# Windowed attention with a routed expert network on one Trainium2 core: other transfer sizes and places for v and the first w1, conversions behind copies, spin matmuls in the start

## The chip, the core and the metric

The kernel runs on one core of a Trainium2 chip. The time is device microseconds of one execution, from the first to the last activity of the core. The kernel before took 225.32 us (median of 3 runs, 225.25 to 226.03). The profile that is read here is of one more execution, of 225.92 us.

## What is computed

Eight sequences ("batches") of 576 rows go through windowed causal attention with 8 heads of 64 columns. The heads are put side by side into x (576 x 512 per batch). The mean over x's rows picks one of eight experts for the whole batch, and this expert's two matrices turn x into the output.

```python
scores = scale * q @ k.T                     # per batch and head, 576 x 576
scores = where(0 <= row - col < 64, scores, -1e9)
x = softmax(scores) @ v                      # heads side by side: 576 x 512
e = argmax(x.mean(rows) @ w_gate)            # one expert for a batch
out = gate_weight * (relu(x @ w1[e]) @ w2[e])   # w1 512 x 1024, w2 1024 x 512
```

## The kernel before, in words

**Units.** The attention of a batch is cut into two units of four heads; unit u belongs to batch u // 2. `load_qk(u)` fetches q and k of a unit on GpSimd's software DMA queue (they become bf16 on the way). `transpose_qk` turns them on TensorE, `leave_qk` copies the result out of PSUM (q always on ScalarE, k on ScalarE or VectorE), `scores` makes three tiles of scores and their exponentials (ScalarE, L397), `values` multiplies by v, and `norm` divides by the row sums and writes x (VectorE, L439 and L441).

**v.** `load_v(b)` fetches the v of a whole batch, 1.18 MB in runs of 256 bytes, on SyncE's hardware DMA queue, in the order in which SyncE meets the transfers; the stores of the output stand in the same queue. Before each transfer GpSimd writes one element of the tile (`memset`, or a copy from the tile given as `behind`), so that the transfer starts no earlier than that. Three tiles serve for v in turn. The conversion of a unit's half of v to f16 has three parts in `cast_part`: "whole" (vn to va, L323), "low" and "high" (va to vb, shifted by half a block of rows). All of them run on VectorE before the change. The fourth batch's v (b = 3) comes in two transfers: blocks 0 to 19 with `load_v(3, part=20)` at L749, and the rest with `load_rest` at L802, behind the second half of batch 1's w1.

**Gate and experts.** `gate(b)` makes the eight logits with one matmul (gl, L501), copies them to SBUF (glog, L505), takes their maximum and its index on VectorE and hands the index to GpSimd, which loads it into a register and issues the loads of w1 and w2 of that expert. For batches 0 and 1 `load_w1` brings w1 in two halves of 512 columns. `expert_up` makes one of eight blocks of the hidden layer (php, L570; relu on ScalarE, L574), `expert_down` one of five blocks of the output (pso, L584 and L601), copied to ob (L311) and stored.

**Order.** Each engine works through its instructions in the order of the program, and that order is written by hand: a preamble for units 0 to 3 (L707 to L779), then a loop over t = 4 to 19, in which a step holds the attention of unit t and slices of the experts' work (`experts(pace)`). In even steps `next_gate` runs the gate of batch t // 2 - 1. `busy(n)` runs n matmuls on a constant tile, whose result nobody reads. PSUM has four tiles of two banks for everything on TensorE, so a tile can start only when an earlier one has been emptied.

Of the kernel before, what the change touches and what calls it, by code (L numbers as in the profile page):

```python
# [9 lines left out]
FP32 = mybir.dt.float32  # L10
# [146 lines left out]
def kernel(  # L157
# [10 lines left out]
    nc = tc.nc  # L168
    B, H, S, D = q.shape
# [10 lines left out]
    def P(ins):  # L180
        tc.keep_in_program_order(ins)
        return ins
# [33 lines left out]

    v_tiles = {}

    def load_v(b, behind=None, part=0):
        vn = vpool.tile([128, NM, D], FP32, tag="vn")  # L220
        if behind is None:

            P(nc.gpsimd.memset(vn[:, 0, 0:1], 0.0))
        else:

            P(nc.gpsimd.tensor_copy(out=vn[:, 0, 0:1], in_=behind))
        v_tiles[b] = vn
        if part:
            P(nc.sync.dma_start(out=vn[:, 0:part, :], in_=vv[b][:, 0:part, :]))
        else:  # L230
            P(nc.sync.dma_start(out=vn, in_=vv[b]))

    def load_rest(b, part, behind):
        vn = v_tiles[b]
        P(nc.gpsimd.tensor_copy(out=vn[:, part, 0:1], in_=behind))
        P(nc.sync.dma_start(out=vn[:, part:NM, :], in_=vv[b][:, part:NM, :]))

    HM = NM // 2

# [238 lines left out]
    w1e = moe_w1.rearrange("e (g p kl) f -> e p g kl f", p=128, kl=2)  # L478
    w1c = moe_w1.rearrange("e (kb p) f -> e p kb f", p=128)
    w2e = moe_w2.rearrange("e (g p i) d -> e p g i d", p=128, i=4)  # L480

    gparts = {}

# [15 lines left out]
    def gate(b):  # L499
        gl = psum.tile([128, 2, 512], FP32, tag="ps", name="gl")  # L500
        P(nc.tensor.matmul(out=gl[:, 0, 0:E], lhsT=onesf, rhs=gparts[b],  # L501
                           start=True, stop=True))

        glog = small.tile([128, E], FP32, tag="glog")
        P(nc.vector.tensor_copy(out=glog, in_=gl[:, 0, 0:E]))  # L505
        gmx = small.tile([128, 8], FP32, tag="gmx")
        P(nc.vector.max(out=gmx, in_=glog))
# [12 lines left out]
        weights[b] = (wpool.tile([128, KB, F], FP16, tag="w1t", name=f"w1t{b}"),  # L520
                      wpool.tile([128, FB, Dm], FP16, tag="w2t", name=f"w2t{b}"))
# [8 lines left out]

    experts_of = {}

    NQ = 2

    def w1_parts(b):
        return weights[b][0].rearrange("p k f -> p (k f)").rearrange(
            "p (h k f) -> p h k f", h=NQ, k=KB)

    def load_w1(b):
        if b < 2:  # L540

            src = w1c[experts_of[b]].squeeze(0)
            for hf in range(NQ):
                P(nc.gpsimd.dma_start(out=w1_parts(b)[:, hf],
                                      in_=src[:, :, ts(hf, F // NQ)]))
        else:
            P(nc.gpsimd.dma_start(  # L547
                out=weights[b][0].rearrange("p (g kl) f -> p g kl f", kl=2),
                in_=w1e[experts_of[b]].squeeze(0)))

    def load_w2(b):
        P(nc.gpsimd.dma_start(
            out=weights[b][1].rearrange("p (g i) d -> p g i d", i=4),
            in_=w2e[experts_of[b]].squeeze(0)))

    h_tiles = {}

    def expert_up(b, ft):
        if b < 2:
            w1t, cols = w1_parts(b)[:, ft // 4], slice(ft % 4, 512, 4)  # L560
# [157 lines left out]
        scores(0, c)  # L718
    make_masks()
    transpose_qk(1, 0)  # L720
    transpose_qk(1, 1, leave=False)
    leave_qk(1, 1, A)
    load_qk(3)
    load_qk(4)
    cast_v(0)
    cast_v(1)
    for c in range(3):
        add_outside(1, c)
    for c in range(3):
        scores(1, c)  # L730
    values(0, 0)
# [5 lines left out]
    pool_mm(0)  # L737
    transpose_qk(2, 1, leave=False)
    leave_qk(2, 1, A)
    busy(1)  # L740
    pool_mm(1)
    pool_parts()
    gate(0)
    load_w1(0)
    load_w2(0)
    load_qk(5)
    load_v(2, w1_parts(0)[:, 0, 0, 0:1])
    load_qk(6)
    load_v(3, part=20)  # L749
    for c in range(3):  # L750
        scores(2, c)
        if c == 0:
# [28 lines left out]
    for t in range(START + 1, NU + LAG):  # L781
# [3 lines left out]
        def next_gate():  # L785
# [81 lines left out]


# [35 lines left out]
```

## Time and profile before

| what | value |
|---|---|
| time, median of 3 runs | 225.32 us (225.25 to 226.03) |
| the profiled execution | 225.92 us, of which the span is 224.0 us |
| TensorE matmul busy | 201.1 us, 90% of the span |
| ScalarE, VectorE, GpSimd busy | 134.2, 128.6, 39.1 us |
| DMA | 45.64 MB written, mean 204 GB/s |
| mean granted TensorE clock | 0.972 |

All places in time are microseconds from the span's start. In the timeline a row gives start, duration, engine, source line, operation, what it writes and reads, how often (x), and in brackets how long the engine stood idle before it and what ended that. In a table of windows the first columns are the busy time of the engines, then come the granted clock of TensorE, the share of the 16 DMA engines and GB/s. Rows of DMA issues end with the size and the time from issue to landing.

### The profile page before, as it was taken

The numbers are of one execution on the slowest core, as the hardware profiler recorded it, in microseconds if no ns is written. First come the engines' busy times: TensorE is split into PE (matmuls) and PEld (weight loads), VectorE is DVE, ScalarE is ACT, GpSimd is POOL, SyncE is SP. The second block draws the span as 40 slices with busy tenths as digits, with TensorE's granted clock in tenths as the row PEclk, the third lists the DMA queues.
The fourth block names the chain that finished last, engine by engine and source line by source line (L and its number), as shares of the span: only waits on it lengthen the run. The fifth ranks groups of instructions, "written<-read, shape, count | busy, mean of one in ns | idle before, by whom it ended". The sixth has DMA issues, their size and how long they took to land.

```text
span 224.0 us, 6996 instructions
## 1 busy us (share of the span) xinstructions
PE 201.1 (90%) x3012; PEld 141.4 (63%) x3012; DVE 128.6 (57%) x310; ACT 134.2 (60%) x221; POOL 39.1 (17%) x69
## 2 busy tenths in 40 slices
PE   7859759999799897999999999999999998999960
PEld 2437638856586556865696658775777567569520
DVE  2538696557866665576774769395939373330120
ACT  2275695964768464785769476968495656417300
POOL 7170161053000700034000700050002000200000
PEclk9976999999999999999999999999999999999995
DMA  5999899999999999999999999999956990699141
GB/s 69 243 256 246 149 157 219 242 251 235 257 225 203 236 223 244 230 288 217 244 227 277 218 231 235 250 264 219 246 141 113 212 266 5 97 225 263 52 136 41
DMA packets 34310, 45.64 MB, mean 204 GB/s; under 512 B 7136, under 2 KB 26720, under 8 KB 34272
## 3 DMA queue, kind: packets, MB, share of 16 engines
q0 software_dynamic: 14624, 26.22, 65.3%
q1 hardware_dynamic: 18704, 18.75, 28.9%
q8 instruction: 25, 0.41, 0.7%
q10 hardware_dynamic: 944, 0.16, 0.4%
q14 instruction: 13, 0.11, 0.1%
HBM read 61.90 MB, written 9.44 MB: 318 GB/s over the span
## 4 chain that ended last, share of the span: by engine, by line
PE 64%; DMA 12%; ACT 11%; DVE 6%; issue 2%; POOL 1%; POOLq 0%
PE php L570 26%; PE pso L584 20%; DMA w1t<-in_moe_w_dram 8%; PE tp L342 6%; ACT xT L470 5%; DMA kn<-in_k_dram 4%; PE op L425 4%; ACT hT L574 4%; PE sp L382 2%; PE pso L601 2%; ACT pt L397 2%; DVE x L441 1%; PE tp L462 1%; DVE vb L311 1%; PE gl L501 1%
## 5 line engine op out<-in xcount | busy, mean ns | idle before, releaser
L570 PE MATMUL php<-xT,w1t 128*128 128x288 f16 x512 | 70.0, 287 | 3.4 <-DMA w1t<-in_moe_w_dram 2.3
L574 ACT ACTIVATE hT<-php,gatew 128x576 f16<-128x576 f32 x64 | 47.2, 744 | 28.8 <-PE php L570 28.6
L570 PEld LDWEIGHTS <-w1t 128*128 128x128 f16 x512 | 56.0, 115 | 10.0 <-DMA w1t<-in_moe_w_dram 2.9
L584 PE MATMUL pso<-w2t,hT 128*128 128x512 f16 x256 | 60.2, 380 | 0.2
L397 ACT ACTIVATE pt<-sp 128x768 f16<-128x768 f32 x48 | 36.4, 817 | 7.5 <-PE sp L382 7.5
L584 PEld LDWEIGHTS <-hT 128*128 128x128 f16 x256 | 23.3, 98 | 26.1 <-issue 1.2
L311 DVE COPY ob<-pso 128x512 f32<-128x512 f32 x23 | 15.9, 690 | 22.9 <-PE pso L584 22.7
L441 DVE TENSOR_TENSOR x<-op,linv 128x640 f16<-128x640 f32 x32 | 26.4, 825 | 1.1
L404 DVE TENSOR_TENSOR pt<-pt,masks 128x768 f16<-128x768 f16 x42 | 22.6, 554 | 5.7 <-ACT pt L397 4.7
L355 ACT COPY dst<-tp 128x1152 bf16<-128x1152 bf16 x16 | 18.0, 1124 | 11.9 <-PE tp L342 11.7
L547 POOL DMA_DIRECT2D w1t<-in_moe_w_dram x6 | 4.4, 729 | 112.8 <-DVE pt L404 91.5
L470 ACT ACTIVATE xT<-tp 128x576 f16<-128x576 f16 x28 | 17.9, 646 | 9.2 <-PE tp L462 9.2
L425 PE MATMUL op<-vb,pt 128*64 128x65 f16 x320 | 16.2, 198 | 0.8 <-DVE ob L311 0.7
L311 DVE COPY vb<-va 64x1152 f16<-64x1152 f16 (+1 forms) x32 | 15.9, 498 | 0.5
L425 PEld LDWEIGHTS <-pt 128*64 128x64 f16 x640 | 13.9, 114 | 3.3 <-issue 2.4
L425 PE MATMUL op<-va,pt 128*64 128x65 f16 x320 | 15.9, 198 | 0.0
L382 PE MATMUL sp<-dst 64*64 64x128 bf16 (+1 forms) x672 | 14.2, 218 | 1.9 <-ACT dst L309 1.2
L382 PEld LDWEIGHTS <-dst 64*64 64x64 bf16 x672 | 10.3, 110 | 8.7 <-issue 4.5
L311 DVE CAST va<-vn 128x1152 f16<-128x1152 f32 x16 | 12.2, 763 | 6.2 <-DMA vn<-in_v_dram 6.1
L493 DVE SCALAR_TENSOR_TENSOR gpart<-wg,pooled,gpart 128x8 f32<-128x8 f32 x21 | 4.8, 226 | 18.4 <-ACT xT L470 18.1
L342 PE MATMUL tp<-ident,kn 128*64 128x128 bf16 x288 | 11.5, 227 | 1.9 <-DMA kn<-in_k_dram 1.9
L342 PEld LDWEIGHTS <-kn 128*64 128x64 bf16 x288 | 9.0, 113 | 6.0 <-issue 3.5
(74 smaller groups left out, 178.5 us busy)
## 6 DMA issues: line engine op xcount, KB each, us to landing
w2t<-in_moe_w_dram POOLq DMA_DIRECT2D x8, 1024.0 KB, 17.6
out_dram<-ob SPq DMA_DIRECT2D x31, 256.0 KB, 8.1
w1t<-in_moe_w_dram POOLq DMA_DIRECT2D x6, 1024.0 KB, 9.4
qn<-in_q_dram POOLq DMA_DIRECT2D x16, 288.0 KB, 13.2
kn<-in_k_dram POOLq DMA_DIRECT2D x16, 288.0 KB, 14.3
w1t<-in_moe_w_dram POOLq DMA_DIRECT2D x4, 512.0 KB, 8.3
out_dram<-ob SPq DMA_DIRECT2D x16, 64.0 KB, 7.3
vn<-in_v_dram SPq DMA_DIRECT2D x1, 640.0 KB, 21.1
```

The lines of the kernel that those rows point to most:

```text
L311: P(eng.tensor_copy(out=out, in_=in_))
L342: P(nc.tensor.transpose(out=tp[64 * s:64 * s + 64, ts(t, 128)], in_=src[:, s, ts(t, D)], identity=ident, tile_position=(0, 64 * s)))
L355: P(nc.scalar.copy(out=dst.rearrange("p (x r t) -> p x r t", x=2, t=NT), in_=view))
L382: P(nc.tensor.matmul(out=sp[64 * half:64 * half + 64, s, 64 * (qblk - 6 * c):64 * (qblk - 6 * c) + n], lhsT=kT[64 * s:64 * s + 64, ts(kblk ...
L397: P(nc.scalar.activation(out=pt, in_=sp[:, :, 0:384], func=AF.Exp, scale=scale))
L404: P(nc.vector.tensor_tensor(out=pt, in0=pt, in1=masks[:, c].rearrange("p s g w -> p s (g w)"), op=ALU.mult))
L425: P(nc.tensor.matmul(out=op[64 * half:64 * half + 64, xx, 65 * jj:65 * jj + 65], lhsT=pt[:, s, 64 * (g % 6):64 * (g % 6) + 64], rhs=win, s ...
L441: P(nc.vector.tensor_tensor(out=x[:, :, h0 * D:(h0 + 2) * D].rearrange("p j (x c) -> p x j c", x=2), in0=view[:, :, :, 0:64], in1=li[:, :, ...
L470: P(nc.scalar.activation(out=xT[:, kb, :], in_=tp[:, kl, 0:S], func=AF.Copy, accum_out=pooled[:, b, kb:kb + 1]))
L570: P(nc.tensor.matmul(out=php[:, sc, 0:288], lhsT=w1t[:, kb, cols], rhs=xT[:, kb, ts(sc, 288)], start=(kb == 0), stop=(kb == KB - 1)))
L574: P(nc.scalar.activation(out=hT[:, ft].rearrange("p (sc s) -> p sc s", sc=2), in_=php[:, :, 0:288], func=AF.Relu, scale=gatew[:, b:b + 1]))
L584: P(nc.tensor.matmul(out=pso[:, 0, :], lhsT=hT[:, fb, ts(mt, 128)], rhs=w2t[:, fb, :], start=(fb == 0), stop=(fb == FB - 1)))
```

## The change

It has seven parts.

1. The v of batch 3 is one transfer at the place of its first part; `load_rest` goes away.
2. The v of batch 4 is issued in step 4, behind the loads of batch 1's w1 and w2, no longer at the end of step 5. The v of batch 2 waits for the second piece of the first w1 (before: for its first half, which holds the same columns).
3. The w1 of batch 0 comes in three pieces of 256, 256 and 512 columns; the rows of hidden units are dealt out by 2 in place of 4 for this batch, so that w2's load has runs of 4 KB in place of 8 KB.
4. In step 4 the conversion of unit 5's v stands behind the next two slices of expert work.
5. The "whole" part of unit 1's v is converted on ScalarE.
6. For batch 0 the logits are read from PSUM, without the copy to glog.
7. Two of unit 1's three `add_outside` and a `busy(2)` stand ahead of the transposes of unit 1's k; `busy(1)` ahead of `pool_mm(1)` is now `busy(3)`, and a `busy(2)` stands ahead of the first gate.

```diff
-    def load_v(b, behind=None, part=0):
+    def load_v(b, behind=None):
...
-        if part:
-            P(nc.sync.dma_start(out=vn[:, 0:part, :], in_=vv[b][:, 0:part, :]))
-        else:
-            P(nc.sync.dma_start(out=vn, in_=vv[b]))
-
-    def load_rest(b, part, behind):
-        vn = v_tiles[b]
-        P(nc.gpsimd.tensor_copy(out=vn[:, part, 0:1], in_=behind))
-        P(nc.sync.dma_start(out=vn[:, part:NM, :], in_=vv[b][:, part:NM, :]))
+        P(nc.sync.dma_start(out=vn, in_=vv[b]))
...
-        glog = small.tile([128, E], FP32, tag="glog")
-        P(nc.vector.tensor_copy(out=glog, in_=gl[:, 0, 0:E]))
+        if b:
+            glog = small.tile([128, E], FP32, tag="glog")
+            P(nc.vector.tensor_copy(out=glog, in_=gl[:, 0, 0:E]))
+        else:
+            glog = gl[:, 0, 0:E]
...
+    PARTS = (((0, 256), (256, 256), (512, 512)), ((0, 512), (512, 512)))
+
+    def w1_part(b, i):
+        lo, n = PARTS[b][i]
+        return weights[b][0].rearrange("p k f -> p (k f)")[
+            :, KB * lo:KB * (lo + n)].rearrange("p (k f) -> p k f", k=KB)
...
-            for hf in range(NQ):
-                P(nc.gpsimd.dma_start(out=w1_parts(b)[:, hf],
-                                      in_=src[:, :, ts(hf, F // NQ)]))
+            for i, (lo, n) in enumerate(PARTS[b]):
+                P(nc.gpsimd.dma_start(out=w1_part(b, i), in_=src[:, :, lo:lo + n]))
...
     transpose_qk(1, 0)
+    add_outside(1, 0)
+    add_outside(1, 1)
+    busy(2)
     transpose_qk(1, 1, leave=False)
...
-    cast_v(1)
-    for c in range(3):
-        add_outside(1, c)
+    cast_part(1, "whole", A)
+    cast_part(1, "low")
+    cast_part(1, "high")
+    add_outside(1, 2)
...
-    busy(1)
+    busy(3)
     pool_mm(1)
     pool_parts()
+    busy(2)
     gate(0)
     load_w1(0)
     load_w2(0)
     load_qk(5)
-    load_v(2, w1_parts(0)[:, 0, 0, 0:1])
+    load_v(2, w1_part(0, 1)[:, 0, 0:1])
     load_qk(6)
-    load_v(3, part=20)
+    load_v(3)
...
-            if START + 1 < t and t // 2 + 2 < B:
+            if t // 2 + 2 < B:
                 load_v(t // 2 + 2)
...
-        if t == START + 2:
-
-            load_rest(3, 20, w1_parts(1)[:, 1, 0, 0:1])
...
-        if t in (4, 5):
+        if t == START + 2:
             cast_v(t + 1)
-        if t == START + 2:
-            load_v(4)
...
         experts(pace)
         experts(pace)
+        if late:
+
+            cast_v(t + 1)
```

How the rows move on the engines is shown at three places. The line numbers of the changed kernel are its own.

VectorE, preamble, before: the conversions of units 0 and 1 (va_120 and vb_122 are the f16 copies of v for even batches) up to the first norm.

```order
L311 COPY va_120<-vn 128x18x64
L311 COPY vb_122<-va_120 64x18x64
L311 COPY vb_122<-va_120 64x17x64
L311 COPY va_120<-vn 128x18x64
L311 COPY vb_122<-va_120 64x18x64 x2
L439 RECIPROCAL linv<-op 128x10
```

The same place of the changed kernel.

```order
L303 COPY va_120<-vn 128x18x64
L303 COPY vb_122<-va_120 64x18x64
L303 COPY vb_122<-va_120 64x17x64
L303 COPY vb_122<-va_120 64x18x64 x2
L431 RECIPROCAL linv<-op 128x10
```

The second copy from vn is gone from VectorE; it stands on ScalarE between the copy of unit 1's k and unit 1's exponentials.

GpSimd, from the gate of batch 0 (eidx is the expert's index) to the mark ahead of batch 2's v, before.

```order
L518 TENSOR_LOAD eidx
L544 ISA
L544 DMA w1t_574<-in_moe_w_dram 128x4x512
L544 ISA
L544 DMA w1t_574<-in_moe_w_dram 128x4x512
L552 ISA
L552 DMA w2t_575<-in_moe_w_dram 128x2x2048
L211 DMA qn<-in_q_dram 128x2x576
L214 DMA kn<-in_k_dram 128x2x576
L226 COPY vn<-w1t_574 128x1
```

The changed kernel, from the same place.

```order
L514 TENSOR_LOAD eidx
L542 ISA
L542 DMA w1t_580<-in_moe_w_dram 128x4x256
L542 ISA
L542 DMA w1t_580<-in_moe_w_dram 128x4x256
L542 ISA
L542 DMA w1t_580<-in_moe_w_dram 128x4x512
L550 ISA
L550 DMA w2t_581<-in_moe_w_dram 128x4x1024
L211 DMA qn<-in_q_dram 128x2x576
L214 DMA kn<-in_k_dram 128x2x576
L226 COPY vn<-w1t_580 128x1
```

One more transfer stands ahead of w2 and of everything behind it on this queue.

VectorE at the end of step 4, before: the last norms of unit 4, the conversion of unit 5's v, and a block of batch 0's output (ob) that leaves PSUM (pso).

```order
L441 TENSOR_TENSOR x_1213<-op,linv 128x2x5x64
L311 COPY va_120<-vn 128x18x64
L311 COPY vb_122<-va_120 64x18x64 x2
L311 COPY ob<-pso 128x512
L489 TENSOR_SCALAR gpart_1295<-wg,pooled 128x8
```

The changed kernel at this place.

```order
L433 TENSOR_TENSOR x_1223<-op,linv 128x2x5x64
L303 COPY ob<-pso 128x512
L303 COPY va_120<-vn 128x18x64
L303 COPY vb_122<-va_120 64x18x64 x2
L482 TENSOR_SCALAR gpart_1303<-wg,pooled 128x8
```

The copy out of PSUM now stands ahead of the conversion.

More of the change, by code (lines that the diff above doesn't have):

```diff
@@ L480 @@
     w2e = moe_w2.rearrange("e (g p i) d -> e p g i d", p=128, i=4)
+    w2f = moe_w2.rearrange("e (g p i) d -> e p g i d", p=128, i=2)
     gparts = {}
@@ L531 @@
     experts_of = {}
[L533 to L537, printed above, removed]
+    PARTS = (((0, 256), (256, 256), (512, 512)), ((0, 512), (512, 512)))
[3 more added lines that the diff above has]
+            :, KB * lo:KB * (lo + n)].rearrange("p (k f) -> p k f", k=KB)
     def load_w1(b):
@@ L552, in load_w2 @@
         P(nc.gpsimd.dma_start(
-            out=weights[b][1].rearrange("p (g i) d -> p g i d", i=4),
-            in_=w2e[experts_of[b]].squeeze(0)))
+            out=weights[b][1].rearrange("p (g i) d -> p g i d", i=4 if b else 2),
+            in_=(w2e if b else w2f)[experts_of[b]].squeeze(0)))
     h_tiles = {}
     def expert_up(b, ft):
-        if b < 2:
-            w1t, cols = w1_parts(b)[:, ft // 4], slice(ft % 4, 512, 4)
+        if b == 0:
+            part = min(ft // 2, 2)
+            at = 256 * (ft // 2) - PARTS[b][part][0]
+            w1t, cols = w1_part(b, part), slice(at + ft % 2, at + 256, 2)
+        elif b == 1:
+            w1t, cols = w1_part(b, ft // 4), slice(ft % 4, 512, 4)
         else:
```

## The prediction

> **What bounds the kernel now.** I read the page first: who is busy, and where TensorE and the DMA engines have holes.
>
> ```profile
> PE 201.1 (90%) x3012; PEld 141.4 (63%) x3012; DVE 128.6 (57%) x310; ACT 134.2 (60%) x221; POOL 39.1 (17%) x69
> DMA  5999899999999999999999999999956990699141
> ```
>
> TensorE (PE) is busy for 90% of the span, and the DMA engines are full in nearly every slice up to three quarters of it. So both can be the bound, and a gain must pass both. Next I went through TensorE's timeline for its idle time. These rows carry nearly all that the change can touch.
>
> ```profile
> 12.03 0.69 PE L342 MATMUL tp<-ident,qn 128*64 128x128 bf16 x18 [0.89 <-DMA qn<-in_q_dram]
> 14.36 1.17 PE L342 MATMUL tp<-ident,kn 128*64 128x128 bf16 x18 [1.64 <-DMA kn<-in_k_dram]
> 24.53 0.36 PE L501 MATMUL gl<-gpart,onesf 128*128 128x8 f32 x2 [0.61 <-DVE gpart L703]
> 28.91 0.81 PE L677 MATMUL idle<-spin 128*128 128x512 bf16 x3 [0.38 <-ACT xT L309]
> 30.95 0.71 PE L382 MATMUL sp<-dst 64*64 64x64 bf16 x42 [1.24 <-ACT dst L309]
> 32.53 2.15 PE L570 MATMUL php<-xT,w1t 128*128 128x288 f16 x16 [0.87 <-DMA w1t<-in_moe_w_dram]
> 59.04 1.14 PE L570 MATMUL php<-xT,w1t 128*128 128x288 f16 x8 [1.00 <-ACT xT L470]
> 76.78 0.19 PE L425 MATMUL op<-vb,pt 128*64 128x65 f16 x1 [0.75 <-DVE ob L311]
> 85.46 1.17 PE L570 MATMUL php<-xT,w1t 128*128 128x288 f16 x8 [1.45 <-DMA w1t<-in_moe_w_dram]
> ```
>
> The first expert matmul (php) starts at 32.53; ahead of it the start is a chain over unit 1, the gate and the first w1. Later there are three waits, 1.00 + 0.75 + 1.45 = 3.20 us. The third view is the table of windows, for the clock.
>
> ```profile
> 10.20:13.60 3.40, 1.40 (x60) 1.11 (x60) 1.18 (x7) 2.76 (x4) 2.87 (x5) 1.00 1.15 260
> 13.60:20.40 6.80, 6.04 (x120) 4.45 (x122) 4.30 (x9) 3.80 (x5) 1.68 (x3) 0.50 1.17 248
> 27.24:30.66 3.42, 2.10 (x39) 1.27 (x38) 3.21 (x7) 3.42 (x5) 3.42 (x5) 1.00 0.63 85
> ```
>
> After a stretch with 1.40 us of matmuls in 3.40 us the granted clock is 0.50 until 20.4; a stretch with 2.10 in 3.42 kept 1.00. The same 18 transposes took 0.69 us before and 1.17 us after the drop.
>
> **The start, step by step.** Unit 1's k lands when it did, since nothing ahead of it changes, so its transposes still begin at 14.36. In the hole ahead of them there are now four matmuls of 384 columns and two of 512. The row at 28.91 gives 0.27 us for one of 512 columns, so together they are at most 0.54 + 4 x 0.20 = 1.35 us, begun at 12.03 + 0.69 = 12.72. They fit in front of 14.36. Until 13.6 they add some 0.88 us: 1.40 + 0.88 = 2.28 of 3.40 us, more than the stretch that kept its clock. I take it that the clock stays up.
>
> The rule that I weigh against this is in the Trainium skill, TensorE: Matmul & The Clock Gate, Part 1: the clock is halved after a whole idle window of about 3.4 us. By it the longest gap here, 1.64 us, would have cost nothing. The trace does not agree (0.50 behind gaps of 0.89 and 1.64), and the trace decides. The page also says that the window runs free of the kernel; whether a fill helps would then change from run to run, which is a rival below.
>
> ```profile
> 15.23 0.76 DVE L311 CAST va<-vn 128x1152 f16<-128x1152 f32 x1 [3.85 <-DMA vn<-in_v_dram]
> 17.00 0.76 DVE L311 CAST va<-vn 128x1152 f16<-128x1152 f32 x1
> 17.79 0.92 DVE L311 COPY vb<-va 64x1152 f16<-64x1152 f16 x2
> 19.40 0.22 DVE L439 RECIPROCAL linv<-op 128x10 f32<-128x10 f32 x1 [0.69 <-PE op L425]
> 22.76 0.82 DVE L441 TENSOR_TENSOR x<-op,linv 128x640 f16<-128x640 f32 x1
> 15.57 1.12 ACT L309 COPY dst<-tp 128x1152 bf16<-128x1152 bf16 x1 [1.50 <-PE tp L342]
> 18.09 2.22 ACT L397 ACTIVATE pt<-sp 128x768 f16<-128x768 f32 x3 [1.40 <-PE sp L382]
> ```
>
> With 0.69 in place of 1.17 us ScalarE's copy of k runs from 15.1 to 16.2. Behind it comes the conversion that VectorE gave away. No row shows ScalarE converting from f32 in SBUF; its bounds are VectorE's 0.76 and ScalarE's 1.12 for as many elements, and I take 1.12: done at 17.3. Unit 1's exponentials start then and not at 18.09, 0.76 earlier, although they stand behind more work, because they waited 1.40 us for TensorE. VectorE does its last two copies at 17.3 to 18.25 (before: to 18.71), and the four norms, 22.76 + 0.82 - 19.40 = 4.18 us back to back, start at about 18.3 and not at 19.40, if TensorE has the values by then. So x is complete 0.76 to 1.1 us earlier; I take 1.0.
>
> ```profile
> 24.93 0.17 DVE L505 COPY glog<-gl 128x8 f32<-128x8 f32 x1 [0.54 <-PE gl L501]
> 25.13 0.17 DVE L507 MAX8 gmx<-glog 128x8 f32<-128x8 f32 x1
> 27.01 1.51 POOL L544 DMA_DIRECT2D w1t<-in_moe_w_dram  x2 [11.73 <-DVE gatew L529]
> w1t<-in_moe_w_dram POOLq DMA_DIRECT2D x1, 512.0 KB, 5.5
> w1t<-in_moe_w_dram POOLq DMA_DIRECT2D x1, 512.0 KB, 7.5
> ```
>
> Without the copy to glog the gate is 25.13 - 24.93 = 0.2 us shorter. The four added spin matmuls near it, 4 x 0.27 = 1.1 us, stand in front of waits (the gate's 0.61 among them); what sticks out I put at 0.2. The gate thus comes 1.0 us earlier, the first w1 at 26.0. Its halves landed at 27.01 + 5.5 = 32.5 and 27.76 + 7.5 = 35.3 (issued 0.75 apart), so a half costs 2.8 us of transfer and a quarter about 1.4: the first piece lands at 26.0 + 5.5 - 1.4 = 30.1. TensorE isn't ready by then. Its last scores before php waited for ScalarE, whose whole chain follows the gate: 30.95 - 1.0 + 0.71 = 30.66. So php starts at about 30.7, **1.7 to 1.8 us earlier**; if quarters were no faster than halves, 1.0. I take 1.7. The second quarter lands where the half would and the last piece at 34.3 or a little later, both ahead of the third and fifth block.
>
> The skill's DMA: Bandwidth & Descriptors, Anatomy of one DMA, gives about 2.0 us for any transfer plus bytes / 436 GB/s. By that a quarter saves only 0.6 us (an estimate) and lands at 30.9; the sum would be 0.2 less. The halves' 2.8 us speak for the larger saving.
>
> **Conversion behind the copy, 59.04.**
>
> ```profile
> 56.71 0.75 DVE L311 CAST va<-vn 128x1152 f16<-128x1152 f32 x1
> 58.45 0.69 DVE L311 COPY ob<-pso 128x512 f32<-128x512 f32 x1
> ```
>
> The copy that frees a PSUM tile waited for three conversions, 58.45 - 56.71 = 1.74 us. It now ends at 57.4 and not at 59.14, and php can take that tile as soon as its scores are through. The 1.00 us goes, but the next block then waits for a tile that the exponentials free: I keep **0.75** (bounds 0 and 1.00).
>
> **Batch 3's v whole and early, 76.78.**
>
> ```profile
> 75.28 0.86 DVE L311 CAST va<-vn 128x1152 f16<-128x1152 f32 x1 [1.98 <-DMA vn<-in_v_dram]
> 76.06 0.67 DVE L311 COPY ob<-pso 128x512 f32<-128x512 f32 x1
> ```
>
> VectorE waited 1.98 us for the rest of that v, and the copy behind it kept TensorE waiting 0.75 us.
>
> ```profile
> q0 software_dynamic: 917, 1.01, 72.7%
> q1 hardware_dynamic: 920, 0.94, 42.2%
> ```
>
> These are the two queues from 40 to 48: GpSimd's (q0) and SyncE's (q1) both had work and took turns, packet by packet, 1.95 MB in 8 us; as q0 converts f32 to 16 bits, nearly 3 MB read. At q1's 0.94 MB in 8 us the v of batches 2 and 3, 2.36 MB from about 32 on, is through by 53, or 57 with the first packets' way: long before 75.28. **0.65** of the 0.75 goes; the copy still follows its own matmuls (bounds 0 and 0.75).
>
> **Batch 4's v beside batch 1's w1, 85.46.**
>
> ```profile
> 73.40 0.72 POOL L547 DMA_DIRECT2D w1t<-in_moe_w_dram  x1 [12.34 <-DVE pt L404]
> q1 hardware_dynamic: 958, 0.89, 112.0%
> q0 software_dynamic: 2, 0.01, 1.0%
> ```
>
> The two last rows are the queues from 74 to 78. Batch 2's w1 was issued at 73.40, and in these 4 us its queue moved 2 packets, while SyncE's moved 0.89 MB of batch 4's v, alone, 0.22 MB in a microsecond. With that v gone from here w1 can start at 74 to 75 and not at 78, and v in its new place is mixed with other loads, as from 40 to 48.
>
> ```profile
> 47.24 1.50 POOL L544 DMA_DIRECT2D w1t<-in_moe_w_dram  x2 [12.67 <-DVE pt L404]
> w1t<-in_moe_w_dram POOLq DMA_DIRECT2D x1, 512.0 KB, 9.0
> ```
>
> Batch 1's first half landed at 47.24 + 9.0 = 56.2, ahead of its use at 59.04; issued 1.7 us earlier and with as much beside it as before, it lands at about 54.5 to 55.5 for a use at 56.3. SyncE now issues batch 0's stores behind this v; there are ten ob tiles and a batch fills five, so nobody waits for the late ones. Of the 1.45 us I count **1.0**, as TensorE arrives 1.7 + 0.75 + 0.65 = 3.1 us earlier at this place and w1 3 to 4 us (bounds 0 and 1.45).
>
> **The sum** is 1.7 + 0.75 + 0.65 + 1.0 = 4.1 us on an execution of 225.92 us: 221.8. That execution was 0.6 above the median of the runs, so I say 225.32 - 4.1 = **221.2**. With each term at its upper bound it is 225.32 - 5.0 = 220.3.
>
> **Rivals.** *The DMA queue takes it back.*
>
> ```profile
> 98.96 0.72 POOL L547 DMA_DIRECT2D w1t<-in_moe_w_dram  x1 [21.19 <-DVE pt L404]
> w1t<-in_moe_w_dram POOLq DMA_DIRECT2D x1, 1024.0 KB, 9.7
> 109.91 2.15 PE L570 MATMUL php<-xT,w1t 128*128 128x288 f16 x16
> ```
>
> Batch 3's w1 landed at 108.7 for a use at 109.91: 1.2 us of slack. If the stream of loads as a whole comes only the gate's 1.0 us earlier, TensorE can keep 2.2 us: 223.1. For it: DMA is full all along. Against it: the two stretches in which v ran alone go. Chance 0.17.
>
> *The clock.* The drop only moves, as the window's phase would have it, and the spin matmuls near the gate last twice as long: 0.2 us from glog and the quarter's part are left, about 0.8 in place of 1.7, and a first w1 that is late eats some of the rest: 222.3. Chance 0.14.
>
> *Slower: batch 1's w1 is held back as batch 2's was.* If q0 runs dry before w1's packets are there, and v then runs alone until it is through, up to 2 MB of two batches' v stand ahead: 9 us at 0.22 MB in a microsecond from about 48.5, so that the first half lands at about 62 (2.8 us and the last packets' way), 3 us behind its use at 59.04 before. With 0.65 and 1.0 still gained: 225.3 + 1.4 = 226.7. It decides when that half lands later than 56.3. For it: the rows at 74 to 78. Against: q0 still has unit 6's q and k to move at the time of the issue. Chance 0.13.
>
> *Little comes of it:* the pieces and the fill shift waits without removing them, and only the glog copy and part of one wait are gained: 224.8. Chance 0.08.
>
> **Chances and range.** The forecast has 0.48, its own range is 220.3 to 222.3. A measurement of this kernel can tell about 0.5% (1.1 us) from no change. Faster by more than that: nearly all of the forecast, the clock's rival and most of the first, 0.47 + 0.14 + 0.15 = 0.76; within 0.5%: 0.12; slower: 0.12. The range reaches from 219.8, half a microsecond below all upper bounds together, to 225.0, and leaves out the slower case, some of the last and a little below: 0.2.
>
> **What would show it.** Right: granted clock 1.00 throughout 13.6 to 20.4; the first w1 issued at 26.0 and php at 30.7; no idle time before php of batch 1; no wait of a conversion for v near 72; php of batch 2 at about 81. Wrong: a clock of 0.50 after 17; a wait for w1 before batch 1's php; a wait for w1 of a microsecond or more at batch 3 or 5.

## The result, and the profile after

The changed kernel takes 223.53 us (median of 9 runs, 221.93 to 224.59); the kernel before, on the same chip, 225.25 us (9 runs, 224.91 to 226.03). The ratio is 0.990, with a 95% interval from 0.988 to 0.993. So it is faster, by 1.7 us from median to median and by about 2.2 us if one goes by the ratio; the forecast was 4.1 us, a time of 221.2. The profiled execution took 223.88 us, with a span of 222.2. The ratios here and below are to runs of the kernel before on the same chip and leave out runs that lie over 1.5% above the fastest of their kernel, while the medians hold all runs, so that the two part where a kernel spreads widely.

TensorE is as busy as before, and so are the DMA engines up to three quarters of the span.

```profile
PE 200.7 (90%) x3018; PEld 139.6 (63%) x3018; DVE 127.9 (58%) x308; ACT 134.8 (61%) x222; POOL 40.2 (18%) x69
...
DMA  5999999999999999999999999999947980699131
```

TensorE's timeline, at the places of which the prediction spoke:

```profile
12.02 0.69 PE L334 MATMUL tp<-ident,qn 128*64 128x128 bf16 x18
12.64 0.99 PE L361 MATMUL sp<-outside,ident 128*128 128x384 bf16 x4
13.85 0.59 PE L679 MATMUL idle<-spin 128*128 128x512 bf16 x2 [0.22 <-ACT pt L389]
14.49 0.69 PE L334 MATMUL tp<-ident,kn 128*64 128x128 bf16 x18
...
29.76 0.71 PE L374 MATMUL sp<-dst 64*64 64x64 bf16 x42 [1.24 <-ACT dst L301]
30.85 2.13 PE L572 MATMUL php<-xT,w1t 128*128 128x288 f16 x16 [0.38 <-DMA w1t<-in_moe_w_dram]
...
56.49 1.17 PE L572 MATMUL php<-xT,w1t 128*128 128x288 f16 x8 [0.19 <-DMA w1t<-in_moe_w_dram]
...
82.16 1.17 PE L572 MATMUL php<-xT,w1t 128*128 128x288 f16 x8 [1.87 <-DMA w1t<-in_moe_w_dram]
83.26 0.42 PE L374 MATMUL sp<-dst 64*64 64x64 bf16 x14
83.61 2.11 PE L572 MATMUL php<-xT,w1t 128*128 128x288 f16 x8
85.65 1.17 PE L334 MATMUL tp<-ident,kn 128*64 128x128 bf16 x18
...
108.04 1.17 PE L572 MATMUL php<-xT,w1t 128*128 128x288 f16 x8
```

The first php of the batches is a ladder on which the gain can be read. Batches 0 to 3 started at 32.53, 59.04, 85.46 and 109.91; they now start at 30.85, 56.49, 82.16 and 108.04. That is 1.68, 2.55, 3.30 and then only **1.87** us earlier, and from there it stays at 1.86 to 1.87. So up to batch 2 most of the forecast is there, and between batches 2 and 3 1.43 us are given back. The rows say where: the wait for batch 2's w1 has not shrunk but grown, from 1.45 to 1.87, and just behind it eight matmuls take 2.11 us that took 1.17 in the row above, and the 18 transposes 1.17 in place of 0.69. The table of windows shows the clock (the last three columns are granted clock, DMA share and GB/s):

```profile
10.20:13.60 3.40, 2.56 (x66) 1.51 (x65) 1.92 (x7) 2.02 (x3) 2.13 (x4) 1.00 1.14 251
13.60:20.40 6.80, 4.93 (x156) 3.40 (x156) 4.53 (x9) 6.24 (x8) 2.52 (x4) 1.00 1.13 247
...
80.02:83.43 3.41, 1.54 (x23) 0.99 (x22) 1.94 (x4) 0.85 (x3) 0.00 (x0) 1.00 1.11 239
83.43:86.85 3.42, 3.42 (x50) 2.31 (x42) 1.38 (x3) 2.12 (x3) 0.00 (x0) 0.50 1.16 247
```

The halved clock is gone from the start, as forecast, and is back behind the wait at batch 2: 1.54 us of matmuls in 3.41, then 3.42 us at 0.50.

### The profile page after: what moved, and what is told of

It is laid out like the page before. It is cut to its first block, busy times and chain, and to the rows that moved or that the text cites. A ratio compares the mean times of both kernels' runs of the same rounds, so it can differ in the third digit from the quotient of the medians.

```text
span 222.2 us, 7005 instructions
## 1 busy us (share of the span) xinstructions
PE 200.7 (90%) x3018; PEld 139.6 (63%) x3018; DVE 127.9 (58%) x308; ACT 134.8 (61%) x222; POOL 40.2 (18%) x69
## 4 chain that ended last, share of the span: by engine, by line
PE 65%; ACT 14%; DMA 10%; DVE 5%; issue 2%; POOLq 0%; POOL 0%
PE php L572 26%; PE pso L586 21%; DMA w1t<-in_moe_w_dram 7%; PE tp L334 6%; ACT xT L462 5%; ACT pt L389 4%; ACT hT L576 4%; PE op L417 4%; DMA kn<-in_k_dram 3%; PE sp L374 2%; PE pso L603 2%; PE tp L454 1%; DVE vb L303 1%; PE gl L494 1%; DVE ob L303 1%
## 5 line engine op out<-in xcount | busy, mean ns | idle before, releaser
L572 PE MATMUL php<-xT,w1t 128*128 128x288 f16 x512 | 70.9, 290 | 2.6 <-DMA w1t<-in_moe_w_dram 2.4
L572 PEld LDWEIGHTS <-w1t 128*128 128x128 f16 x512 | 55.3, 114 | 10.6 <-DMA w1t<-in_moe_w_dram 3.2
L417 PE MATMUL op<-vb,pt 128*64 128x65 f16 x320 | 15.7, 196 | 0.6 <-ACT pt L389 0.6
L417 PEld LDWEIGHTS <-pt 128*64 128x64 f16 x640 | 13.4, 111 | 3.0 <-issue 1.8
L486 DVE SCALAR_TENSOR_TENSOR gpart<-wg,pooled,gpart 128x8 f32<-128x8 f32 x21 | 4.8, 227 | 18.3 <-ACT xT L462 18.0
L303 DVE CAST va<-vn 128x1152 f16<-128x1152 f32 x15 | 11.6, 770 | 4.3 <-DMA vn<-in_v_dram 4.2
```

What stands on the lines that cost most here:

```text
L303: P(eng.tensor_copy(out=out, in_=in_))
L417: P(nc.tensor.matmul(out=op[64 * half:64 * half + 64, xx, 65 * jj:65 * jj + 65], lhsT=pt[:, s, 64 * (g % 6):64 * (g % 6) + 64], rhs=win, s ...
L572: P(nc.tensor.matmul(out=php[:, sc, 0:288], lhsT=w1t[:, kb, cols], rhs=xT[:, kb, ts(sc, 288)], start=(kb == 0), stop=(kb == KB - 1)))
```

## The experiments

Two theories stood against each other. **C, the clock:** what is missing was lost to that halved window. **D, the stream of loads:** the DMA engines are full, batch 2's w1 comes when the bytes ahead of it are through, and what TensorE gains ahead of it turns into waiting. As a rival to D stood **Q**: batch 0's stores, queued behind two v, had taken v's place in the hole of GpSimd's queue. Each edit is to the changed kernel unless it says otherwise.

**The wait at batch 2 filled.**

```diff
+        if b == 2 and ft == 0:
+            for _ in range(6):
+                P(nc.tensor.matmul(out=php[:, 0, :], lhsT=spin[:, 0:128], rhs=spin,
+                                   start=True, stop=True))
```

> The changed kernel with six spin matmuls of 512 columns (6 x 0.27 = 1.6 us) put into the PSUM tile of batch 2's first php, ahead of it, where TensorE waits 1.87 us for w1 until 82.16. Theory C (the clock): that wait is followed by 3.41 us at a granted clock of 0.50 (83.43 to 86.84), which costs about 1.5 us and comes in some runs and not in others; filled, the clock stays 1.00 there, php of batch 3 starts at about 106.5 and not 108.04, the median falls by 1.0 to 1.5 us to about 222.2 and the runs spread by less than 1 us (now 2.7). Theory D (the stream of loads takes it back): php of batch 3 waits for its w1 and starts at about 108 again; median 223.5. Rival: the spin matmuls themselves hold php back, 223.8 or more.

222.45 us (6 runs, 221.25 to 222.82), ratio 0.986 (0.982 to 0.990). This execution had a halved window in the start instead (16.00 to 19.41 with 1.83 us of small matmuls, then 0.50), so php of batch 0 came at 31.82; the step from batch 2 to batch 3 is what counts.

```profile
81.22 1.46 PE L572 MATMUL php<-spin 128*128 128x512 bf16 x5
83.06 1.17 PE L576 MATMUL php<-xT,w1t 128*128 128x288 f16 x8 [0.39 <-DMA w1t<-in_moe_w_dram]
...
107.67 1.54 PE L576 MATMUL php<-xT,w1t 128*128 128x288 f16 x11
```

107.67 - 83.06 = 24.61 us, against 108.04 - 82.16 = 25.88. The clock stayed at 1.00 and 1.27 us of this step came back, where 1.5 had been expected: C holds for the step. php of batch 3 came no earlier than 107.67 because its w1 landed at 107.62, so there the loads bind again. The median is 1.1 us below the changed kernel's, as C had it, but the intervals of the two ratios meet. The runs still spread by 1.6 us, not by less than 1.

**Batch 0's stores on GpSimd's queue.**

```diff
-            P(nc.sync.dma_start(out=out[b, ts(mt, 128), :], in_=ob))
+            P((nc.gpsimd if b == 0 else nc.sync).dma_start(out=out[b, ts(mt, 128), :], in_=ob))
```

(The two stores of the last block likewise.)

> The changed kernel with batch 0's stores issued on GpSimd's software queue and not on SyncE's. Theory Q (the stores): batch 2's w1, issued at 71.00, landed as late as 82.11 because batch 0's stores had queued behind two v and moved alone in the hole of the software queue; with the stores out of there w1 lands by 80.3 or earlier, php of batch 2 starts at about 80.3 without a wait and no half clock follows: 223.5 - 1.9 - 1.0 = about 220.6. Rival R (the lag belongs to the software queue itself, or to its backlog): w1 still lands at 82, php at 82.2, median 223.5. If GpSimd's waits for the stores delay its other issues (batch 4's q and k), some units wait for k: slower than 223.5.

222.78 us (12 runs), ratio 0.990 (0.987 to 0.992).

```profile
82.12 1.17 PE L572 MATMUL php<-xT,w1t 128*128 128x288 f16 x8 [2.09 <-DMA w1t<-in_moe_w_dram]
```

The stores were out of SyncE's queue, which moved nothing but 0.03 MB from 72 to 75, and w1 landed at the same 82.1, though it was issued 0.9 us later (71.91). Q falls: GpSimd's queue moved 0.65 MB from 72 to 75, a backlog of its own that stood ahead of w1. A halved window followed again (php of batch 3 at 108.01).

**Batch 4's v late again.**

```diff
-            if t // 2 + 2 < B:
+            if START + 1 < t and t // 2 + 2 < B:
                 load_v(t // 2 + 2)
...
         if t == START + 2:
             cast_v(t + 1)
+            load_v(4)
```

> The changed kernel with batch 4's v issued at the end of step 5 again (the fourth term of the prediction undone). The prediction: batch 2's w1 waits behind that v, alone from 74 to 78, as before the change; php of batch 2 starts about 1.0 us later, at 83.2; median about 224.5. Theory Q: the stores of batch 0 then go early, and v takes their place in the hole, so that w1 comes 0 to 1 us later than 82.11: 223.5 to 224.5. Rival: the move of v was itself the loss, php of batch 2 at 81 or earlier, median 222.5.

223.82 us (12 runs), ratio 0.992 (0.988 to 0.995).

```profile
83.11 1.17 PE L572 MATMUL php<-xT,w1t 128*128 128x288 f16 x8 [2.10 <-DMA w1t<-in_moe_w_dram]
```

The 83.11 looks like the prediction's, but here the first w1 was issued at 26.59 and not at 25.65. From there to w1 of batch 2 it is 56.5 us in both. So the place of this v gave w1 nothing, and the ratios of the two kernels do not tell them apart either. It serves another user: late, v lands at 84.8, and VectorE waits.

```profile
84.92 0.76 DVE L303 CAST va<-vn 128x1152 f16<-128x1152 f32 x1 [4.53 <-DMA vn<-in_v_dram]
```

In the changed kernel that conversion ran at 79.58 without a wait. The step from batch 2 to batch 3 is 26.0 us here with a clock of 1.00 throughout: 1.5 us more than 24.5.

**Only the conversion behind the copy** (an edit to the kernel before: unit 5's `cast_v` moved behind the next two slices of expert work).

> The kernel before with one part of the change: unit 5's conversion of v behind the copy that empties the PSUM tile. The prediction: 0.75 us less (bounds 0 and 1.00), php of batch 1 at 58.2 and not 59.04; this stays if the wait at batch 2 for w1 (issued by a gate that comes as much earlier) does not grow: 224.5. Rival: w1 of batch 2 lands at the same 85.4, the wait grows by 0.75 and nothing is left: 225.25.

224.98 us (12 runs) against 225.50 (29 runs), ratio 0.999 (0.996 to 1.003).

```profile
57.06 1.17 PE L570 MATMUL php<-xT,w1t 128*128 128x288 f16 x8
...
75.88 0.19 PE L425 MATMUL op<-vb,pt 128*64 128x65 f16 x1 [1.46 <-DVE ob L311]
...
84.33 0.93 PE L570 MATMUL php<-xT,w1t 128*128 128x288 f16 x6 [1.21 <-DMA w1t<-in_moe_w_dram]
```

Batch 0 to batch 1 takes 57.06 - 31.62 = 25.44 us in place of 26.51: the 1.0 us is gone. But the wait for the rest of batch 3's v doubles from 0.75 to 1.46, and at batch 2 only 0.2 us are left (52.71 in place of 52.93 from batch 0). Alone the part is worth nothing that shows.

**The rest of batch 4's v, and batch 5's, behind batch 2's w1.**

```diff
-    def load_v(b, behind=None):
+    def load_v(b, behind=None, part=NM):
...
-        P(nc.sync.dma_start(out=vn, in_=vv[b]))
+        P(nc.sync.dma_start(out=vn[:, 0:part, :], in_=vv[b][:, 0:part, :]))
...
+            if t == START + 3:
+                load_rest(4, 18, weights[2][0][:, 0, 0:1])
             if t // 2 + 2 < B:
-                load_v(t // 2 + 2)
+                load_v(t // 2 + 2, part=18 if t == START + 1 else NM)
```

> The changed kernel with batch 4's v in two transfers: blocks 0 to 17 where it is issued now, blocks 18 to 35 (0.59 MB) and batch 5's v only when batch 2's w1 has landed. Theory D (the stream of loads, now with its place: from the first w1 to batch 2's w1 the DMA engines are full and move 12.5 to 12.8 MB in every variant so far, at 0.23 to 0.24 MB in a microsecond, so only bytes that are put behind that w1 bring it earlier): 0.59 / 0.238 = 2.5 us less ahead of it, it lands at 79.6, php of batch 2 starts at about 80.3 without a wait, no half clock behind it, and batch 3's w1, which has all these bytes ahead of it again, becomes the next limit: php of batch 3 at 106 to 107, median 221.5 to 222.3. Rival R (the lag belongs to the software queue): w1 lands at 82, wait and median as in the changed kernel, 223.5.

222.75 us (6 runs), ratio 0.989 (0.986 to 0.993); the profiled execution has the shortest span of all, 219.8. The packets from 3 us behind the issue of the first w1 to the landing of batch 2's, first of this kernel, then of the changed one, then of the one before:

```profile
DMA packets 11182, 11.96 MB, mean 229 GB/s; under 512 B 2711, under 2 KB 9637, under 8 KB 11173
```

```profile
DMA packets 10201, 12.70 MB, mean 237 GB/s; under 512 B 400, under 2 KB 8656, under 8 KB 10192
```

```profile
DMA packets 13120, 12.77 MB, mean 230 GB/s; under 512 B 5008, under 2 KB 11831, under 8 KB 13111
```

With 0.74 MB less ahead of it w1 landed 55.2 us behind the issue of the first w1 and not 56.5, and the wait fell to 1.05 (php at 80.42). That is half of what was expected: the v in two transfers brought 2,300 more packets under 512 bytes, and the rate fell from 237 to 229 GB/s. D holds in direction: w1 moved with the bytes, where neither queue nor place had moved it. This rests on one profile. Batch 3's w1 became the next limit, as expected (php at 105.45, a wait of 0.15).

**The fills of the start taken out** (spin matmuls and `add_outside` at their old numbers and places).

> The changed kernel without the fills of the start: the spin matmuls and the two add_outside are back at their old numbers and places. Theory C (the clock is set by windows of 3.41 us that run free of the kernel; a window in which TensorE works for less than about half is followed by one at 0.50): the emptiest 3.41 us of the start go from 45% busy to about 30%, so nearly every run has one or two halved windows there; php of batch 0 starts at 31.5 to 32.5 and not at 30.85, mean clock lower by 0.004 to 0.008, median 224.2 to 224.5. Rival: the spin matmuls cost as much as they keep, or the wait for w1 at batch 2 swallows what the start loses: 223.5 or less.

223.09 us (6 runs), ratio 0.990 (0.987 to 0.994).

```profile
10.98:14.39 3.41, 1.05 (x50) 0.76 (x36) 0.61 (x4) 3.23 (x4) 3.22 (x5) 1.00 1.15 250
14.39:17.81 3.42, 3.08 (x24) 1.67 (x24) 1.84 (x3) 1.86 (x2) 1.09 (x2) 0.50 1.14 254
...
79.25:82.66 3.41, 2.12 (x32) 0.85 (x21) 2.34 (x6) 2.63 (x6) 0.00 (x0) 1.00 1.04 228
82.66:86.08 3.42, 2.92 (x46) 2.31 (x47) 0.64 (x2) 1.71 (x3) 0.00 (x0) 1.00 1.16 247
```

php of batch 0 came at 31.92, and the mean clock of the runs is 0.976 where the changed kernel's is 0.984, both as C has it. But the median is no higher. At batch 2 TensorE waited 1.80 us, nearly as long as in the changed kernel, with php at 83.16; here the edge of a window (82.66) cut the wait in two, 2.12 us of matmuls were left in the first part, and no halving followed: php of batch 3 came at 107.68, ahead of 108.04. What the fills keep in the start is 1.07 us of a profile and does not show in the median. Nor do they keep it always: of the eleven profiles with them, seven have no halved window ahead of php of batch 0 and four have at least one (that of the filled wait at batch 2 is among the four); the three profiles without them (the kernel before, the one with the conversion alone, and this one) have two each.

**The first w1 in two halves again** (PARTS of batch 0 as of batch 1, w2's layout with it).

> The changed kernel with the first w1 in two halves again (w2's layout with it). The prediction: a quarter lands 1.4 us ahead of a half, so that php of batch 0 starts 0.7 to 1.0 us later with halves, 31.7, median 224.3. By the changed kernel's trace (a quarter took 5.15 us from issue to landing, a half 5.48): php of batch 0 at about 31.2. Theory D: batch 2's w1 still decides there, and what batch 0 loses is lost from that wait; median 223.5 within 0.3.

222.89 us (6 runs), ratio 0.988 (0.984 to 0.992): no worse than quarters.

```profile
31.82 1.39 PE L568 MATMUL php<-xT,w1t 128*128 128x288 f16 x5 [0.58 <-DMA w1t<-in_moe_w_dram]
```

```profile
82.85 1.17 PE L568 MATMUL php<-xT,w1t 128*128 128x288 f16 x8
```

TensorE waited 0.58 us for the half (issued 26.43, landed 31.78). Batch 2's w1 landed 56.4 us behind the first issue, as in the changed kernel, TensorE came there later, and the wait was gone, as D has it. TensorE's lateness is not the halves' alone, though: this execution had halved windows from 10.94 to 14.35 and from 31.42 to 34.83.

**Unit 1's whole conversion back on VectorE** (`cast_part(1, "whole")` without the A).

> The changed kernel with unit 1's whole conversion back on VectorE. The prediction: ScalarE's conversion brought x 0.76 to 1.1 us earlier; undone, the gate issues the first w1 at 26.5 and not at 25.65, php of batch 0 starts at about 31.6, and as all loads start with that gate, batch 2's w1 lands 0.8 later too: median 224.3. Rival: the conversion lies beside TensorE's own work, nothing moves: 223.5.

223.63 us (12 runs), ratio 0.991 (0.988 to 0.994).

```profile
31.17 1.03 PE L572 MATMUL php<-xT,w1t 128*128 128x288 f16 x7
```

The first w1 was issued at 26.42, 0.77 later, as expected; php of batch 0 came only 0.3 later, since it no longer waited for w1 (this first quarter took 4.0 us to land, the changed kernel's 5.15), and batch 2's w1 0.44 later. The medians don't tell the two apart.

**Batch 3's v in two transfers, back to back.**

```diff
-        P(nc.sync.dma_start(out=vn, in_=vv[b]))
+        if b == 3:
+            P(nc.sync.dma_start(out=vn[:, 0:20, :], in_=vv[b][:, 0:20, :]))
+            P(nc.sync.dma_start(out=vn[:, 20:NM, :], in_=vv[b][:, 20:NM, :]))
+        else:
+            P(nc.sync.dma_start(out=vn, in_=vv[b]))
```

> The changed kernel with batch 3's v in two transfers again (blocks 0 to 19 and 20 to 35), one right behind the other and with no new wait, so that order and bytes stay. Theory P (packets): a v in parts moves in packets of 256 bytes (4,608 more packets under 512 bytes in the kernel before and in the one with batch 4's v in parts), a whole v in packets of 1 KB or more, and the small ones cost the full DMA engines about 1.8 us; batch 2's w1 then lands 58.0 to 58.4 us behind the issue of the first w1, as before the change, and not 56.0 to 56.5 as in the variants with whole v; php of batch 2 starts 1.5 to 2 us later, median 224.5 to 225. Rival V (the prediction's: it was the place of batch 4's v): 56.0 to 56.5 us, median 223.5 within 0.4.

226.23 us (12 runs: one of 222.30, eleven of 225.18 to 227.46), ratio 0.995 (0.990 to 1.000). Eleven runs are slower than any of the changed kernel's, but the intervals of the two ratios still meet, so the size of the loss is not sure. Batch 2's w1 landed 59.9 us behind the first issue, later than P had it, and in this profile the loss came another way. The queues from 52 to 56, of this kernel and of the changed one:

```profile
DMA packets 1238, 0.81 MB, mean 202 GB/s; under 512 B 634, under 2 KB 1227, under 8 KB 1238
...
q0 software_dynamic: 629, 0.65, 94.9%
q1 hardware_dynamic: 609, 0.16, 29.0%
```

```profile
DMA packets 976, 0.98 MB, mean 245 GB/s; under 512 B 20, under 2 KB 976, under 8 KB 976
...
q0 software_dynamic: 497, 0.49, 72.8%
q1 hardware_dynamic: 479, 0.49, 44.0%
```

Both queues had nearly as many packets each, 629 and 609 or 497 and 479. A packet of 256 bytes takes a turn as one of 1 KB does, so v in parts moved 0.16 MB where the whole v moved 0.49. The first 20 blocks landed at 69.6, VectorE waited for them, and the gate behind it on VectorE was late, so that batch 2's w1 was issued at 74.72 and not at 71.00:

```profile
69.71 0.76 DVE L307 CAST va<-vn 128x1152 f16<-128x1152 f32 x1 [5.46 <-DMA vn<-in_v_dram]
```

```profile
72.17 0.56 PE L498 MATMUL gl<-gpart,onesf 128*128 128x8 f32 x2 [4.83 <-DVE gpart L490]
```

**w1 ahead of q and k.**

```diff
             if START + 1 < t < NU - 3:
+                load_qk(t + 2)
                 load_qk(t + 3)
...
-        if t % 2 == 1 and t + 3 < NU:
-            load_qk(t + 3)
```

> The changed kernel with q and k of units 8, 10, 12 and 14 issued one step later, behind w1 of batches 2 to 5 in GpSimd's queue and not ahead of it. Theory D (bytes ahead): 0.59 MB in packets of 1,152 bytes, 512 of them at 106 ns over 16 engines = 3.4 us of DMA time, leave the place ahead of batch 2's w1; it lands about 53.5 us behind the issue of the first w1 (56.5 in the changed kernel), at 79; php of batch 2 starts at 80.3 without a wait and with no half clock behind it, batch 3's w1 comes 2.5 us earlier too, php of batch 3 at about 104.8; median 220.3 to 221.2. Rival: a unit's q and k are late now, or something else binds at batch 3: php of batch 3 at 106 or later, median 222 to 223.5.

227.75 us (12 runs), ratio 1.002 (0.998 to 1.006). The rival came true.

```profile
80.89 1.17 PE L572 MATMUL php<-xT,w1t 128*128 128x288 f16 x8 [0.36 <-DMA w1t<-in_moe_w_dram]
85.54 0.69 PE L334 MATMUL tp<-ident,kn 128*64 128x128 bf16 x18 [2.08 <-DMA kn<-in_k_dram]
```

w1 landed 54.8 us behind the first issue, 1.6 earlier, as fewer bytes would have it; but k of unit 8 was late by 2.08 us, and k of later units too. The same with three more spin matmuls in the start:

> The kernel with w1 ahead of q and k, and three more spin matmuls (0.8 us) ahead of the transposes of unit 0's k, where TensorE waits 1.3 to 1.8 us for k to land and the emptiest 3.41 us of the start are about 45% busy. Theory C: they become about 60% busy, the start has no halved window, mean clock of the runs 0.990 or more and the median 0.3 to 0.8 us below that of the kernel with w1 ahead alone, 219.8 to 220.6. Rival: the spin matmuls push k's transposes back as much as they keep, no difference.

227.01 us (12 runs), ratio 1.000 (0.996 to 1.004): k is late again, and the start shows nothing in the times (the runs' clock lay between 0.976 and 0.995, not at 0.990 or more). This profile also speaks against a plain count of bytes.

```profile
82.07 1.24 PE L572 MATMUL php<-xT,w1t 128*128 128x288 f16 x8 [2.40 <-DMA w1t<-in_moe_w_dram]
```

The queue was as in the run before, but w1 landed 56.8 us behind the first issue, no earlier than with q and k ahead of it. Packets of unit 8's q moved before the last of w1 had; so w1 was not through on all 16 DMA engines at one time. What held its last packets back is not settled.

**Two of the edits together:** the rest of batch 4's v behind batch 2's w1, and four spin matmuls ahead of that php.

> The changed kernel with the rest of batch 4's v behind batch 2's w1, as in the run with that alone, and four spin matmuls (4 x 0.27 = 1.1 us) ahead of batch 2's first php, where 1.05 us of waiting were left. Theory D and C together: php of batch 2 starts at about 81, its wait can no longer take half of a 3.41-us window, no run has a halved window there, php of batch 3 at 105.5 to 106.5 behind its w1 (80.2 us after the issue of the first w1); median 221.5 to 222.3, the runs' clock 0.987 or more. Rival: the spread is not the clock's but that of the first loads, and nothing is gained over the run without spin matmuls: 222.7.

222.09 us (6 runs, 220.42 to 224.19) against 225.35, ratio 0.983 (0.978 to 0.989): the lowest ratio and the lowest single run of all, though its interval meets that of the changed kernel. Its profiled execution, the slowest of the six, had a halved window in the start (php of batch 0 at 31.91) and none at batch 2. There php of batch 2 came at 82.80 and of batch 3 at 108.02, each later than expected, as the first w1 was issued only at 27.17; batch 2's w1 landed 55.6 us behind that, close to the 55.2 of the run with the rest of v alone. Three of the six runs had a clock below the expected 0.987.

Four parts of the change were undone one at a time above: the fills, the quarters, ScalarE's conversion and the place of batch 4's v. The ratios are 0.988 to 0.992, inside the changed kernel's interval, so the times show no worth for any of these alone. The missing copy to glog was not tried by itself.

## Why the prediction was wrong in size

**The start, 1.7 us: right.** php came 1.68 us earlier. Inside the step two sizes were off and cancelled.

```profile
16.24 1.16 ACT L301 CAST va<-vn 128x1152 f16<-128x1152 f32 x1
```

```profile
18.38 0.22 DVE L431 RECIPROCAL linv<-op 128x10 f32<-128x10 f32 x1
```

```profile
25.65 2.24 POOL L542 DMA_DIRECT2D w1t<-in_moe_w_dram  x3 [9.53 <-DVE gatew L525]
...
w1t<-in_moe_w_dram POOLq DMA_DIRECT2D x2, 256.0 KB, 5.4
```

ScalarE's conversion took 1.16 us (taken as 1.12), the norms began at 18.38 (18.3), the gate's issue came at 25.65 (26.0). The first quarter landed at 30.8, not 30.1: 5.15 us behind its issue where a half had taken 5.5. That would be a saving of 0.3 us and not of 1.4, but this profile is the slowest in it: in the ten others with quarters the first landed 3.98 to 5.02 us behind its issue, in eight of them 4.0 to 4.3, and in the three with halves the first half 5.3 to 5.5. So a quarter mostly saves about 1.1 us. The Trainium skill's rule that the prediction had set beside it (DMA: Bandwidth & Descriptors, Anatomy of one DMA) gives 0.6 by estimate; most of these traces lie nearer to the prediction's 1.4. The fill kept the clock in this profile; without it php came 1.07 us later.

**The conversion behind the copy, 0.75 us: right on the ladder** (2.55 - 1.68 = 0.87), wrong as a term of a sum: alone it was eaten by the next waits. The terms are links of one chain and count only as far as the next load allows.

**Batch 3's v whole, 0.65 us: right, and it did more than the prediction gave it.**

```profile
70.76 0.76 DVE L303 CAST va<-vn 128x1152 f16<-128x1152 f32 x1
```

No wait is left there, and TensorE gained 1.17 us between batch 1's php and its arrival at batch 2. And batch 2's w1, which landed 58.4 us behind the first issue before and 58.0 with the conversion alone, lands at 56.0 to 56.5 in the changed kernel and in six variants with whole v, whatever the stores, batch 4's v or the pieces of the first w1 do. The totals above point to the packets: the same 12.7 MB, at 237 in place of 230 GB/s, with 4,600 fewer packets under 512 bytes. This is argued from those totals and not shown; whole v alone in the kernel before was not tried, and with v in two parts the late gate covers it.

**Batch 4's v beside batch 1's w1, 1.0 us: the step that failed.** The prediction read that w1 starts late because v runs alone at that place, took v away, and let w1 come 3 to 4 us earlier and TensorE 3.1. These numbers leave between nothing and 0.9 us for the term, not 1.0. w1 came 3.3 us earlier (85.4 to 82.1) and TensorE 3.7, so the wait grew from 1.45 to 1.87 in place of falling to 0.45: the term is -0.42 us.

That the 3.3 lies within the 3 to 4 is luck, for the place of v did not bring it: 1.4 are the gate's, and the 1.9 that remain, put down to the packets above, are there with v late again too. These are the queues of the changed kernel from 71.5 to 75, the counterpart of the prediction's rows from 74 to 78:

```profile
q1 hardware_dynamic: 621, 0.98, 76.6%
q0 software_dynamic: 187, 0.20, 32.9%
```

v was gone from the hole, but stores filled SyncE's queue, and on GpSimd's q and k of earlier units still stood ahead of w1. By the packets' own records (1,152 bytes each for q and k, 4,096 for w1) the last of q and k moved at 74.64 and the first of w1 at 74.87; with v late again it was 75.99 and 76.02. Before the change 4.5 us lay between the two (73.48 and 77.98), and there v did run alone, as the prediction read. From its first packet to its landing w1 took 7.4 us before and 7.2 after. The DMA engines had been full all along (the prediction had said that a gain must pass both bounds, and then priced this wait by one of them). This is in kind the prediction's rival "the DMA queue takes it back", one batch earlier than that put it. Its 223.1 is near the measured time by luck: at batch 3, where it saw the loss, w1 landed at 105.98 for a use at 108.04, and the loss came from the clock.

**What no step had: the halved window behind that wait.** A wait of 1.45 us leaves 1.96 us of matmuls in a window of 3.41 that holds all of it; one of 1.87 left 1.54. The prediction had the rows to see it (a stretch with 1.40 lost its clock, one with 2.10 kept it) and used them for the start alone; its rival of the clock let the drop move, but within the start. Steps from batch 2 to batch 3 with one halved window took 25.88, 25.89 and 25.67 us, those without 24.45, 24.47, 24.61, 24.52, 24.28 and 24.61: about 1.3 us. (The other five profiles are not in this count: a late v, k or w1 held batch 3 back in them.) Without it, if nothing else had come between, the profile would have been 3.3 us ahead, and the fastest of the nine runs, 221.93 at the highest clock of them (0.990), is 3.3 below 225.25; the slowest, 224.59, has the lowest (0.972). The clock is not all of the spread: six runs of one variant (the rest of v behind w1) lay between 221.53 and 223.59 with four of them at 0.991 to 0.994. What moves those stays open.

**All together.** Of 1.7 + 0.75 + 0.65 + 1.0 = 4.1 us the profile shows 1.68 + 0.87 + 1.17 - 0.42 = 3.30 us up to batch 2, and less the 1.43 behind it 1.87. The measured time lies in the prediction's range, but two terms make up the difference that no step of it had: a wait that grew, and the halved clock behind it. Of its signs of being wrong, which were for the start and for batches 1, 3 and 5, only one showed: batch 1's first half landed at 56.44 and php waited 0.19 us for it. For batch 2, where the loss came, it had named none.

## What to carry to other kernels

Where the DMA engines are full, price a wait for a load by the bytes that pass ahead of it, the size of their packets and their rate, counted from the last point at which the stream was empty, and not by the transfer that is seen beside it; moving one transfer mostly changes who waits. Add up gains along one chain only as far as the next load's landing. And a wait near half a clock window (1.87 of 3.41 us here) can have a second price behind it, so look at what remains of each wait, not only at what goes.

## What had not been expected of the hardware

The granted clock changes on a grid of 3.41 us whose phase differs from run to run: the halved stretch before, 13.60 to 20.40, is two such windows long, the one after, 83.43 to 86.85, one. The page named in the prediction (the Trainium skill, TensorE: Matmul & The Clock Gate, Part 1) has that window and that it runs free of the kernel, and the runs agree: the wait of 1.80 us that lay across an edge cost nothing behind it, the one of 1.87 us inside a window cost 1.3. They differ where the page's table has the clock halved after a whole idle window: windows with 1.05, 1.54 and 1.83 us of matmuls were followed by a halved one, one with 2.12 was not. Busy time alone doesn't draw the line, though: without the fills one with 2.33 us, of small matmuls, was followed by a halved one, and with batch 4's v late one with 1.68 was not.

```profile
21.22:24.63 3.41, 2.33 (x71) 1.92 (x64) 2.39 (x6) 1.66 (x2) 0.00 (x0) 1.00 1.19 227
24.63:28.05 3.42, 3.21 (x62) 3.04 (x62) 2.02 (x9) 2.67 (x6) 1.32 (x2) 0.50 0.57 100
```

```profile
79.34:82.75 3.41, 1.68 (x8) 0.59 (x6) 0.46 (x2) 2.19 (x6) 0.00 (x0) 1.00 1.06 222
82.75:86.17 3.42, 2.57 (x30) 1.98 (x31) 1.25 (x3) 1.85 (x3) 0.00 (x0) 1.00 1.17 247
```

Two queues that both had packets to move took turns packet by packet, whatever a packet's size: from 52 to 56, 609 packets against 629 carried 0.16 against 0.65 MB. A transfer of part of a tile of v moved in 256 bytes a packet, the whole tile in 1 KB, so that cutting it in two cost it two thirds of its share (0.16 in place of 0.49 MB).

A load on GpSimd's queue starts at different distances from its issue. In the kernel before, the first packet of batch 0's w1 moved 1.46 us behind the issue at 27.01, when SyncE's queue was nearly empty, and that of batch 2's w1 4.59 us behind the issue at 73.40, when v streamed alone on SyncE's queue. What the 3 us between them are made of is open.
